# A triangular substitution moved to PSUM beside a four-bank pool, and its blocks stored block by block

## The chip, the cores and the metric

The kernel runs on one core of a Trainium2 chip. The metric is the device time of one execution in microseconds. Before the change it takes 909.23 us in the median of three runs (908.24 to 913.0).

## What is computed

Three stages follow one another. The first is a linear recurrence with a 40x40 state for each of 32 heads (4 batches of 8) over 768 steps:

```
for t in range(S):
    y[:, :, t] = einsum('bhd,bhde->bhe', rt, state)
    Sa = einsum('bhde,bhe->bhd', state, at)
    state = state * wt[:, :, None, :] - einsum('bhd,bhe->bhde', Sa, bt)
    state = state + einsum('bhd,bhe->bhde', vt, kt)
```

Its output, 3072 rows of 320, goes through two mixtures of 8 experts (320 to 1024 to 320, ReLU, the expert with the largest logit, its softmax weight as gate). In the first, rows with a negative skip score pass unchanged and the result is added to the row; in the second an expert takes at most `capacity` rows, and the rest give zero.

## The kernel before

**Tiling.** The recurrence is worked in chunks of 64 steps. A unit (`u`) is one chunk of the 8 heads of one batch; there are 48, and two batches alternate, so unit `u + 2` takes the state that unit `u` leaves. Within a unit the coupling of the steps is a triangular system of 64 rows for each head. Its inverse is put together from two 32x32 triangular blocks on the diagonal, inverted by substitution, and the block between them.

**The substitution.** Four units are a group; its 64 diagonal blocks (8 heads, 4 units, two blocks each) lie on 128 partitions, each block on two: one partition works the even columns of the inverse, the other the odd ones. `nt` holds a block (32x32) on each partition, `xs` its half of the growing inverse (16x32), both in SBUF and both read by VectorE (DVE). `solve_ops` (L277 to 301) is a generator of 62 steps for each group: for each of 31 columns one multiply (L290, the column of `xs` times the row of `nt` into `tmp`), and one add (L295, `tmp` onto `xs` in place). The sizes run from 16 to 136 elements a partition. Only in the first group are the larger steps cut in two.

**How it gets its data.** `scores` (L208) makes a unit's products on PE; ACT copies the negated ones to `abt` (L219), and one DMA stores them as 64 rows of 2048 bytes to `scr` in DRAM (L227). Once a group's four units are stored, `solve_in` (L247) loads `nt` with four DMAs of 32x32 runs of 128 bytes. `solve_new` (L257) makes a fresh `xs`: a memset and two memsets of its diagonal on GpSimd (POOL). At the group's end `solve_out` (L319) stores `xs` to `ttd` in DRAM with two DMAs, and `load_tt` (L329) brings it back as `tt` with four, in the layout that the matmuls need. `load_l21` (L268) loads the block between the diagonal ones from `scr`. All these DMAs are issued on SP's queue, in the order of the program.

**Order of the work.** It is written out by hand: what the program says first is issued first on each engine. `run` (L540) has one pass for each unit, with the units ahead (`v = u + 11`) being prepared beside the current one:

- on top: the DMAs due (`load_pre`, `load_duo`, the list `loads`, `load_post`), the transpose `tnat` of the next unit (L352, DVE, reads `tt`), `c1` and `stran` of this one (PE);
- `xmul` (L508, DVE), `decay` (L437, POOL, writes `spp`), `prep` (two scans on DVE, L177 and L192, around which POOL makes `kb`, L201, and `aks`, L203);
- `scores`, `uu`, `kbtr`, `gg` on PE, with ACT's copies between; `akmask` on POOL (L232, two selects);
- `t21a`, `c2`, `utr` (PE), `gmask` (L488, DVE), `yy` (PE), `state` (L428, DVE), `xx` every second pass, `t21b`.

Between these `fill(n)` puts n steps of the substitution on DVE (16 in a pass), and of smaller chores of the routing. A group's substitution takes up four passes; it ends in the pass with `u % 4 == 1`, its `tt` is loaded in the next pass and read by `tnat` in the one after.

**PSUM.** Eight banks: two for `scores`, `gg` and `warm` (pool `psA`), two shared by `kbtr`, `stran`, `xx` and the routing's counts (`psK`), two by `c1`, `uu`, `t21a`, `t21b`, `utr` (`psC`), and one each for the state's product `ps_s` and the output `ps_y`. The framework gives out the banks of a pool as the program's order frees them and makes the engines wait for the last reader.

**After the recurrence** PE runs the experts, with weights split into two parts, from about 470 us to the end.

Of the kernel before, what the change touches and what calls it, by code (L numbers as in the profile page):

```python
# [66 lines left out]
class Attention:  # L67
    def __init__(self, tc, ctx, aps, moe):
# [15 lines left out]
        self.psA = ep(tc.tile_pool(name="psA", bufs=2, space=P))  # L84
        self.psK = ep(tc.tile_pool(name="psK", bufs=2, space=P))
        self.psC = ep(tc.tile_pool(name="psC", bufs=2, space=P))
        self.psS = ep(tc.tile_pool(name="psS", bufs=1, space=P))

# [18 lines left out]

        self.ps_s = self.psS.tile([128, NP, D], F32, name="ps_s")
        self.ps_y = self.psS.tile([128, NP, C], F32, name="ps_y")
        self.in1b = [early([PR, NP, CW], F32, name=f"in1b{i}") for i in range(2)]  # L110
# [29 lines left out]
        self.warm(W0, zero[:, 0])  # L140
        self.later = [(V, self.ps_s), (V, self.ps_y), (V, self.tt[0]), (V, self.tt[1])]
        self.later += [(A, t[96:128]) for t in self.aks[E0:]]
# [65 lines left out]
    def scores(self, u):  # L208
        nc = self.nc
        X = self.U[u]  # L210
        ps = self.psA.tile([128, NP, 2, C], F32, name="psA")
        aks, kb = X["aks"], X["kb"]
        for p in range(NP):
            nc.tensor.matmul(ps[:, p], kb[:, p].rearrange("p x t -> p (x t)"),  # L214
                             aks[:, p].rearrange("p h t -> p (h t)"), start=True, stop=True)
        if u % 2 == 0:
            self.abt = self.pe.tile([128, NP * 2 * C], F32, name="abt", bufs=2)
        abt = self.abt[u % 2 * 64:u % 2 * 64 + 64]
        nc.scalar.activation(out=abt, in_=ps[64:128].rearrange("p a h t -> p (a h t)"), func=AF.Copy, scale=-1.0)  # L219
        for o, h in ((64, 0), (0, 1)):  # L220
            nc.scalar.copy(out=aks[o:o + 64, :, h], in_=ps[0:64, :, h])
        g = u // GU
        if u % GU == 0:
            scr = self.dr.tile([C, GU, H, C], F32, name="scr")
            self.grp[g] = dict(scr=scr)
        scr = self.grp[g]["scr"]
        nc.sync.dma_start(out=scr[:, u % GU].rearrange("s h t -> s (h t)"), in_=abt)  # L227

# [7 lines left out]
    def kbtr(self, u):  # L236
        nc = self.nc
        X = self.U[u]
        ps = self.psK.tile([128, NP, PR], F32, name="psK")
        for p in range(NP):  # L240
            nc.tensor.transpose(ps[:, p], X["kb"][0:PR, p].rearrange("p x t -> p (x t)"), self.ident[0:PR, 0:PR])
        kbs = self.pl.tile([128, NP, PR], F32, name="kbs", bufs=LEAD + 3)
        nc.scalar.copy(out=kbs, in_=ps)
        X["kbs"] = kbs


    def solve_in(self, g):  # L247
        nc = self.nc
        G = self.grp[g]
        scr = G["scr"].rearrange("s u h t -> s (u h) t")  # L250
        for par in range(2):
            for blk in range(2):
                o = par * 64 + blk * HB
                r = slice(blk * HB, blk * HB + HB)
                nc.sync.dma_start(out=G["nt"][o:o + HB], in_=scr[r, :, r].rearrange("s x t -> x s t"))

    def solve_new(self, G):  # L257
        nc = self.nc
        nt = self.pv.tile([128, HB, HB], F32, name="nt")
        xs = self.pv.tile([128, HB // 2, HB], F32, name="xs")  # L260
        nc.gpsimd.memset(xs, 0.0)
        xf = xs.rearrange("p c t -> p (c t)")
        for par in range(2):
            sl = slice(par * 64, par * 64 + 64)
            nc.gpsimd.memset(xf[sl, par:par + 15 * (HB + 2) + 1:HB + 2], 1.0)
        G.update(xs=xs, nt=nt)

    def load_l21(self, g):  # L268
        nc = self.nc
        G = self.grp[g]  # L270
        scr = G["scr"].rearrange("s u h t -> s (u h) t")
        l21 = self.p2.tile([128, GU * NP, HB], F32, name="l21")
# [4 lines left out]
    def solve_ops(self, g):  # L277
# [4 lines left out]
        def ops():  # L282
            for j in range(HB - 1):
# [13 lines left out]
                if j == HB - 2:  # L297
                    self.solve_out(g)
                yield
# [19 lines left out]
    def solve_out(self, g):  # L319
        nc = self.nc  # L320
        G = self.grp[g]
        xs = G["xs"]
        ttd = self.dr.tile([2 * GU * H, HB, HB], F32, name="ttd")
# [88 lines left out]
    def c2(self, u):  # L412
        nc = self.nc
        X = self.U[u]
        if u // IL % NCH == NCH - 1:
            return
        for p in range(NP):
            for r in (0, 64):
                nc.tensor.matmul(self.ps_s[r:r + D, p], X["kbs"][:, p, r:r + D], X["vu"][:, p, r // 64, 0:D], start=True, stop=True)

# [41 lines left out]
    def stran(self, u):  # L462
        nc = self.nc
        X = self.U[u]
        spp = self.spp[u % (2 * IL)]
        ps = self.psK.tile([128, NP, PR], F32, name="psSt", tag="psK")
        for p in range(NP):
# [22 lines left out]
    def yy(self, u):  # L490
        nc = self.nc
        X = self.U[u]

        for p in range(NP):
            for h in range(2):
                o = h * 64
                nc.tensor.matmul(self.ps_y[o:o + D, p], X["kbs"][:, p, o:o + D], X["g"][:, 2 * p + h],  # L497
                                 start=p == 0, stop=False, skip_group_check=True)
        for p in range(NP):
            for h in range(2):  # L500
                o = h * 64
                nc.tensor.matmul(self.ps_y[o:o + D, p], X["sde"][o:o + D, p], X["r"][o:o + D, h, p],  # L502
                                 start=False, stop=p == NP - 1, skip_group_check=True)

    def xmul(self, u):
        X = self.U[u]
        xt = self.xts[u // 2 % 2]
        self.nc.vector.tensor_tensor(out=xt[0:PR, :, (u % 2) * C:(u % 2) * C + C], in0=self.ps_y[0:PR], in1=X["pp"], op=ALU.mult)  # L508
        del self.U[u]
# [3 lines left out]
    def xx(self):  # L513
        nc = self.nc
        if self.xr is not None:
            t, xt = self.xr
            self.xr = None
            ps = self.psK.tile([128, NP, SELN], F32, name="psX", tag="psK")
            for p in range(NP):
# [20 lines left out]
    def run(self):  # L540
        self.todo, self.aux, self.sinks, self.loads = [], [], [], []
        self.xr, self.rate = None, 0.0
        begin = self.moe.setup()
        begins = [BG0, BG1, BG2] + [GU * g + 4 - LEAD for g in range(3, NG)]
        for u in range(-LEAD - 2, NU):
# [76 lines left out]
            if nxt == 0:  # L622
                self.warm(5, self.grp[0]["xs"].rearrange("p c t -> p (c t)"))
            if isn:
# [8 lines left out]
            for f in places:  # L633
                f()
            self.fill(FC)
            if on:
                self.state(u)
# [24 lines left out]
    def finish(self):  # L662

        self.last, self.placed = [], []
        last = self.psC.tile([128, NP, C], F32, name="psYl", tag="psC")
        self.nc.vector.memset(last, 0.0)
        self.xmul(NU - 3)
# [7 lines left out]
        self.xmul(NU - 2)  # L675
        self.ps_y = last
        self.yy(NU - 1)
# [130 lines left out]
class Moe:  # L808
# [44 lines left out]
    def route(self, rows, lg, valid, T, G, slack=0):  # L853
# [42 lines left out]
        def place():  # L896
            p = self.ps_pool(128, T * W).rearrange("p (t w) -> p t w", w=W)
            nc.tensor.matmul(p, self.tri, ohf, start=True, stop=False)
            nc.tensor.matmul(p, self.one, cs[:, 0:T], start=False, stop=True)
            ps.append(p)  # L900

# [533 lines left out]
def build(tc, aps):  # L1435
    nc = tc.nc
    with ExitStack() as ctx, tc.manual_schedule():
        moe = Moe(tc, ctx, aps)
        with ExitStack() as actx:
            att = Attention(tc, actx, aps, moe)  # L1440
            moe.ps_pool = lambda p, n: att.psK.tile([128, 512], F32, name="psR", tag="psK")[0:p, 0:n]
            att.run()
# [26 lines left out]
```

## Time and profile before

| | |
|---|---|
| median of the runs | 909.23 us |
| the profiled execution | 912.79 us |
| its span, first to last instruction | 911.1 us |
| mean granted clock of PE | 0.906 |
| PE busy | 818.9 us (90%) |
| DVE busy | 670.5 us (74%) |
| ACT busy | 483.7 us (53%) |
| POOL busy | 365.1 us (40%) |
| DMA | 138.45 MB, 199464 packets, 141425 of them under 512 B |

Times are microseconds unless marked ns. PE is the matmul engine, DVE VectorE, ACT ScalarE, POOL GpSimd, SP the queue that issues the DMAs. The profiled execution's span is one execution; a share of busy time is a mean over stages with different limits, so the steady stretch of the recurrence, 100 to 400 us, is read by itself. [...]

### The profile page before, as it was taken

How to read it: one execution, taken by the hardware profiler on the slowest of the kernel's cores; microseconds unless marked ns; L12 is line 12 of the kernel's file. 1: busy time of each engine (PE TensorE's matmuls, PEld its weight loads, DVE VectorE, ACT ScalarE, POOL GpSimd, SP SyncE). 2: the span in 40 equal slices, each digit the busy share in tenths (PEclk: the TensorE clock that was granted, in tenths of full speed). 3: DMA queues.
4: the chain of work that ended last, by engine and by line, in shares of the span. 5: the costliest groups of instructions: out<-in, count | busy, mean ns of one | idle time of the engine just before them, and what ended most of it. 6: DMA issues, size and time to landing. Idle time of an engine off the chain costs nothing.

```text
span 911.1 us, 24122 instructions
## 1 busy us (share of the span) xinstructions
PE 818.9 (90%) x9084; PEld 741.1 (81%) x9084; DVE 670.5 (74%) x1964; ACT 483.7 (53%) x1176; POOL 365.1 (40%) x487
## 2 busy tenths in 40 slices
PE   6657789898798988989999799999988999999995
PEld 5536678787687877878878599999988999999995
DVE  8999888999999999999745558887765444444441
ACT  5834565566566574766554255555634445455541
POOL 5743434445455454553022324334422333333321
PEclk7557797889888897999999799999999999999998
DMA  7989999987888978885573474554624245444310
GB/s 215 227 158 173 178 201 206 166 173 143 174 156 184 179 141 161 169 153 124 111 196 80 134 245 151 176 182 131 201 85 136 96 133 166 117 153 127 116 36 23
DMA packets 199464, 138.45 MB, mean 152 GB/s; under 512 B 141425, under 2 KB 182708, under 8 KB 199344
## 3 DMA queue, kind: packets, MB, share of 16 engines
q1 hardware_dynamic: 196000, 127.04, 61.3%
q0 software_dynamic: 3344, 9.83, 3.2%
q8 instruction: 74, 1.21, 0.6%
q14 instruction: 46, 0.38, 0.2%
HBM read 105.87 MB, written 32.43 MB: 152 GB/s over the span
## 4 chain that ended last, share of the span: by engine, by line
PE 47%; DVE 3%; POOL 2%; issue 2%; ACT 1%; DMA 1%; SPq 0%; POOLq 0%; ACTq 0%; DVEq 0%
PE psH L1154 18%; PE psY L1178 5%; PE psY L1180 5%; PE psY L1179 5%; PE psT L1133 2%; PE psG L481 1%; PE psY L1175 1%; PE psY L1176 1%; PE psR L1208 1%; PE ps_y L502 1%; PE psU L407 1%; PE ps_y L497 1%; PE psX L520 1%; DMA xslots<-rows,si 1%; PE psT L1197 1%
## 5 line engine op out<-in xcount | busy, mean ns | idle before, releaser
L290 DVE TENSOR_TENSOR tmp<-xs,nt 128x126 f32<-128x126 f32 (+27 forms) x391 | 180.8, 466 | 10.1 <-DMA nt<-scr 3.2
L1160 DVE SCALAR_TENSOR_TENSOR hl<-psH,hh 128x256 fp32r<-128x256 f32 (+1 forms) x136 | 64.9, 477 | 88.0 <-ACT hh L1158 86.3
L1158 ACT ACTIVATE hh<-psH 128x256 fp32r<-128x256 f32 (+1 forms) x136 | 61.4, 452 | 114.1 <-PE psH L1154 111.8
L1178 PE MATMUL psY<-w2h,hh 128*128 128x320 f32 x328 | 105.6, 322 | 0.0
L295 DVE TENSOR_TENSOR xs<-xs,tmp 128x126 f32<-128x126 f32 (+27 forms) x391 | 100.0, 260 | 6.7
L1180 PE MATMUL psY<-w2h,hl 128*128 128x320 f32 x328 | 101.8, 310 | 0.0
L1179 PE MATMUL psY<-w2l,hh 128*128 128x320 f32 x328 | 101.7, 310 | 0.0
L1154 PE MATMUL psH<-xh,w1h 128*128 128x256 f32 (+1 forms) x408 | 89.5, 329 | 1.8 <-ACT xh L1136 1.7
L214 PE MATMUL psA<-aks,kb 128*128 128x128 f32 x384 | 69.6, 340 | 22.2 <-POOL aks L203 18.0
L1154 PE MATMUL psH<-xl,w1h 128*128 128x256 f32 (+1 forms) x408 | 86.6, 322 | 0.0
L214 PEld LDWEIGHTS psA<-aks,kb 128*128 128x128 f32 x384 | 62.8, 248 | 25.4 <-POOL aks L203 20.1
L437 POOL TENSOR_TENSOR spp<-s,pc 104x320 f32<-104x320 f32 x44 | 32.2, 732 | 116.9 <-DVE s L428 49.7
L201 POOL TENSOR_TENSOR kb<-pre,q 104x512 f32<-104x512 f32 x40 | 47.4, 1185 | 75.8 <-PE psY L362 16.1
L203 POOL TENSOR_TENSOR aks<-pre,pp 104x512 f32<-104x512 f32 x48 | 58.5, 1219 | 42.8 <-DVE pp L192 34.7
L960 POOL DMA_INDIRECT out<-yo,ix x32 | 35.7, 1117 | 97.8 <-ACT yo L1231 47.4
L1154 PEld LDWEIGHTS psH<-xh,w1h 128*128 128x128 f32 x408 | 67.2, 195 | 5.3 <-ACT xh L1136 2.4
L1154 PEld LDWEIGHTS psH<-xl,w1h 128*128 128x128 f32 x408 | 67.3, 193 | 2.9
L481 PE MATMUL psG<-rb,vd 128*128 128x128 f32 x384 | 56.5, 292 | 11.6 <-DVE g L488 11.6
L1154 PE MATMUL psH<-xh,w1l 128*128 128x256 f32 (+1 forms) x272 | 65.2, 321 | 0.0
L377 ACT COPY tt<-psT 32x128 f32<-32x128 f32 x96 | 24.6, 256 | 75.6 <-PE psT L375 71.7
L1178 PEld LDWEIGHTS psY<-w2h,hh 128*128 128x128 f32 x328 | 62.1, 189 | 0.4
L1179 PEld LDWEIGHTS psY<-w2l,hh 128*128 128x128 f32 x328 | 62.1, 189 | 0.0
(172 smaller groups left out, 2040.5 us busy)
## 6 DMA issues: line engine op xcount, KB each, us to landing
pre<-pre SPq DMA_DIRECT2D x48, 523.2 KB
raw<-w SPq DMA_DIRECT2D x32, 512.0 KB
raw<-w SPq DMA_DIRECT2D x32, 480.0 KB
xslots<-mzero SPq DMA_DIRECT2D x11, 648.0 KB
scr<-abt SPq DMA_DIRECT2D x48, 128.0 KB
nt<-scr SPq DMA_DIRECT2D x48, 128.0 KB
vu<-vu SPq DMA_DIRECT2D x24, 256.0 KB
raw<-w SPq DMA_DIRECT2D x16, 320.0 KB
```

The costliest lines, as they stand in the source:

```text
L201: e.tensor_tensor(out=kb[0:PR].rearrange("p a x t -> p x a t"), in0=kbd, in1=qr.unsqueeze(1).to_broadcast([PR, 2, NP, C]), op=ALU.mult)
L203: nc.gpsimd.tensor_tensor(out=aks[0:PR], in0=a, in1=pp.unsqueeze(2).to_broadcast([PR, NP, 2, C]), op=ALU.mult)
L214: nc.tensor.matmul(ps[:, p], kb[:, p].rearrange("p x t -> p (x t)"), aks[:, p].rearrange("p h t -> p (h t)"), start=True, stop=True)
L290: nc.vector.tensor_tensor(out=tv[:, c:d], in0=xs[:, c:d, j:j + 1].to_broadcast([128, d - c, m]), in1=nt[:, j:j + 1, j + 1:HB].to_broadcast ...
L295: nc.vector.tensor_tensor(out=xs[:, c:d, j + 1:HB], in0=xs[:, c:d, j + 1:HB], in1=tv[:, c:d], op=ALU.add)
L481: nc.tensor.matmul(ps[:, 2 * p:2 * p + 2], vd[:, p].rearrange("q x t -> q (x t)"), r[:, :, p], start=True, stop=True)
L1154: nc.tensor.matmul(ps, a, b, start=j == 0, stop=j == 7)
L1158: nc.scalar.activation(out=hh[:, 0:n], in_=ps, func=AF.Relu)
L1160: nc.vector.scalar_tensor_tensor(out=o, in0=ps[:, s], scalar=0.0, in1=hh[:, s].bitcast(F32), op0=ALU.max, op1=ALU.subtract)
L1178: nc.tensor.matmul(ps[0:m], hh[:, s], bh[:, f], start=f == 0, stop=False)
L1179: nc.tensor.matmul(ps[0:m], hh[:, s], bl[:, f], start=False, stop=False)
L1180: nc.tensor.matmul(ps[0:m], hl[:, s], bh[:, f], start=False, stop=f == KF - 1)
```

## The change

`xs` moves into PSUM, in a pool of two banks (`psI`). Its start is kept once in SBUF (`xs0`), and ACT copies it into the bank for each group (`solve_new`); at the end ACT copies the result to SBUF for the DMAs (`solve_out`), which is now called later in the pass, after the last three fill steps, through the list `outs`. To free the banks, `psK`, `psC` and the two fixed banks become one pool of four, `psC`; the state's product and the output are allocated anew in each pass, and their first matmuls write 64 partitions in place of 40, so that the rows that are read with them are written. The counts of the routing are copied out of PSUM by ACT.

The scores are stored three times: the two diagonal blocks of each head to `scr`, head by head, and the upper 32 rows whole to `top`. `nt` is then loaded with two DMAs of one 4096-byte run a partition, and `l21` from `top`.

```diff
-        self.psK = ep(tc.tile_pool(name="psK", bufs=2, space=P))
-        self.psC = ep(tc.tile_pool(name="psC", bufs=2, space=P))
-        self.psS = ep(tc.tile_pool(name="psS", bufs=1, space=P))
+        self.psI = ep(tc.tile_pool(name="psI", bufs=2, space=P))
+        self.psC = ep(tc.tile_pool(name="psC", bufs=4, space=P))
...
-        self.ps_s = self.psS.tile([128, NP, D], F32, name="ps_s")
-        self.ps_y = self.psS.tile([128, NP, C], F32, name="ps_y")
+        self.xs0 = early([128, HB // 2, HB], F32, name="xs0")
...
+        G.memset(self.xs0, 0.0)
+        xf = self.xs0.rearrange("p c t -> p (c t)")
+        for par in range(2):
+            sl = slice(par * 64, par * 64 + 64)
+            G.memset(xf[sl, par:par + 15 * (HB + 2) + 1:HB + 2], 1.0)
...
-            scr = self.dr.tile([C, GU, H, C], F32, name="scr")
-            self.grp[g] = dict(scr=scr)
-        scr = self.grp[g]["scr"]
-        nc.sync.dma_start(out=scr[:, u % GU].rearrange("s h t -> s (h t)"), in_=abt)
+            scr = self.dr.tile([2, GU * H, HB, HB], F32, name="scr")
+            top = self.dr.tile([HB, GU, H, C], F32, name="top")
+            self.grp[g] = dict(scr=scr, top=top)
+        scr, top = self.grp[g]["scr"], self.grp[g]["top"]
+        for blk in range(2):
+            r = slice(blk * HB, blk * HB + HB)
+            nc.sync.dma_start(out=scr[blk, u % GU * H:u % GU * H + H].rearrange("h s t -> s h t"),
+                              in_=abt[r].rearrange("s (h t) -> s h t", h=H)[:, :, r])
+        nc.sync.dma_start(out=top[:, u % GU].rearrange("s h t -> s (h t)"), in_=abt[0:HB])
...
-        ps = self.psK.tile([128, NP, PR], F32, name="psK")
+        ps = self.psC.tile([128, NP, PR], F32, name="psK", tag="psC")
...
         for par in range(2):
-            for blk in range(2):
-                o = par * 64 + blk * HB
-                r = slice(blk * HB, blk * HB + HB)
-                nc.sync.dma_start(out=G["nt"][o:o + HB], in_=scr[r, :, r].rearrange("s x t -> x s t"))
+            nc.sync.dma_start(out=G["nt"][par * 64:par * 64 + 64], in_=G["scr"].rearrange("b x s t -> (b x) s t"))
...
         nt = self.pv.tile([128, HB, HB], F32, name="nt")
-        xs = self.pv.tile([128, HB // 2, HB], F32, name="xs")
-        nc.gpsimd.memset(xs, 0.0)
-        xf = xs.rearrange("p c t -> p (c t)")
-        for par in range(2):
-            sl = slice(par * 64, par * 64 + 64)
-            nc.gpsimd.memset(xf[sl, par:par + 15 * (HB + 2) + 1:HB + 2], 1.0)
+        xs = self.psI.tile([128, HB // 2, HB], F32, name="psI")
+        nc.scalar.copy(out=xs, in_=self.xs0)
...
                 if j == HB - 2:
-                    self.solve_out(g)
+                    self.outs.append(g)
...
-        xs = G["xs"]
+        xs = self.pv.tile([128, HB // 2, HB], F32, name="xs")
+        nc.scalar.copy(out=xs, in_=G["xs"])
...
+        self.ps_s = self.psC.tile([128, NP, D], F32, name="psS", tag="psC")
         for p in range(NP):
-            for r in (0, 64):
-                nc.tensor.matmul(self.ps_s[r:r + D, p], X["kbs"][:, p, r:r + D], ...)
+            for r, m in ((0, 64), (64, D)):
+                nc.tensor.matmul(self.ps_s[r:r + m, p], X["kbs"][:, p, r:r + m], ...)
...
-        ps = self.psK.tile([128, NP, PR], F32, name="psSt", tag="psK")
+        ps = self.psC.tile([128, NP, PR], F32, name="psSt", tag="psC")
...
+        X["py"] = ps = self.psC.tile([128, NP, C], F32, name="psY", tag="psC")
...
-            ps = self.psK.tile([128, NP, SELN], F32, name="psX", tag="psK")
+            ps = self.psC.tile([128, NP, SELN], F32, name="psX", tag="psC")
...
-                self.warm(5, self.grp[0]["xs"].rearrange("p c t -> p (c t)"))
+                self.warm(5, self.moe.zero[:, 0])
...
             self.fill(FC)
+            for g in self.outs:
+                self.solve_out(g)
+            self.outs = []
...
+            if G == 2 and self.paced:
+                c = t(Q * E, "pc").rearrange("p (t w) -> p t w", w=W)
+                nc.scalar.copy(out=c, in_=p)
+                p = c
```

## Rows read from the trace of the kernel before

**Rows 1.** 100 to 400 us: busy PE, PEld, DVE, ACT, POOL; PE clock; DMA share, GB/s.
```profile
100.00:400.00 300.00, 266.28 (x4214) 233.78 (x4212) 276.88 (x816) 175.55 (x513) 147.79 (x231) 0.87 0.89 171
```
**Rows 2.** Costliest groups: shapes, count, busy us, mean ns, idle before.
```profile
L290 DVE TENSOR_TENSOR tmp<-xs,nt 128x126 f32<-128x126 f32 (+27 forms) x391 | 180.8, 466 | 10.1 <-DMA nt<-scr 3.2
L295 DVE TENSOR_TENSOR xs<-xs,tmp 128x126 f32<-128x126 f32 (+27 forms) x391 | 100.0, 260 | 6.7
```
**Rows 3.** Order of time, DVE and POOL, 253 to 259: start, us, instruction.
```profile
253.20 0.78 POOL L437 TENSOR_TENSOR spp<-s,pc 104x320 f32<-104x320 f32 x1 [2.20 <-DVE xs L295]
253.40 0.65 DVE L290 TENSOR_TENSOR tmp<-xs,nt 128x58 f32<-128x58 f32 x1
...
254.38 0.69 DVE L177 TENSOR_TENSOR_SCAN q<-pre,one 104x264 f32<-104x264 f32 x1
...
255.20 1.17 POOL L201 TENSOR_TENSOR kb<-pre,q 104x512 f32<-104x512 f32 x1 [1.23 <-issue]
255.21 1.23 DVE L290 TENSOR_TENSOR tmp<-xs,nt 128x56 f32<-128x56 f32 x1
256.37 0.69 DVE L192 TENSOR_TENSOR_SCAN pp<-pre,in1b 104x264 f32<-104x264 f32 x1
...
257.14 1.19 POOL L203 TENSOR_TENSOR aks<-pre,pp 104x512 f32<-104x512 f32 x1 [0.77 <-DVE pp L192]
257.20 1.22 DVE L290 TENSOR_TENSOR tmp<-xs,nt 128x81 f32<-128x81 f32 x1
```
**Rows 4.** Groups kept apart by shape, DVE, to 470 us: busy us, mean ns.
```profile
L290 DVE TENSOR_TENSOR tmp<-xs,nt 128x115 f32<-128x115 f32 x11 | 3.0, 270 | 0.1
...
L290 DVE TENSOR_TENSOR tmp<-xs,nt 128x16 f32<-128x16 f32 x12 | 2.1, 175 | 0.3
```
**Rows 5.** Order of time, DVE and POOL, 89 to 93.5 us.
```profile
89.50 0.69 DVE L177 TENSOR_TENSOR_SCAN q<-pre,one 104x264 f32<-104x264 f32 x1
...
90.32 0.16 DVE L290 TENSOR_TENSOR tmp<-xs,nt 128x16 f32<-128x16 f32 x1
90.33 1.20 POOL L201 TENSOR_TENSOR kb<-pre,q 104x512 f32<-104x512 f32 x1 [0.80 <-PE psY L362]
90.44 1.65 DVE L192 TENSOR_TENSOR_SCAN pp<-pre,in1b 104x264 f32<-104x264 f32 x1
...
92.08 0.67 DVE L488 TENSOR_TENSOR g<-psG,cst 128x512 f32<-128x512 f32 x1
92.17 1.19 POOL L203 TENSOR_TENSOR aks<-pre,pp 104x512 f32<-104x512 f32 x1 [0.64 <-DVE xs L295]
92.68 0.72 DVE L290 TENSOR_TENSOR tmp<-xs,nt 128x31 f32<-128x31 f32 x1
```
**Rows 6.** As rows 4: instructions with an operand in PSUM, and one without.
```profile
L928 DVE TENSOR_TENSOR ok<-psR,ok 128x48 f32<-128x48 f32 x6 | 1.2, 201 | 0.7 <-PE psR L899 0.7
L932 DVE TENSOR_TENSOR u<-u,ok 128x48 f32<-128x48 f32 x6 | 1.2, 201 | 0.0
...
L130 DVE MEMSET ps_y<- 128x256 f32 x1 | 0.3, 272 | 0.0
```
**Rows 7.** From the last add to tnat: order of time, a wait's total, ACT's copy.
```profile
251.28 0.18 DVE L295 TENSOR_TENSOR xs<-xs,tmp 128x16 f32<-128x16 f32 x1
...
262.85 0.31 DVE L352 STREAM_TRANSPOSE tn<-tt 96x128 f32<-96x128 f32 x1 [0.31 <-DMA tt<-ttd]
...
DVE tn L352 <- DMA tt<-ttd: 17.5, 10, 3.9
...
L219 ACT ACTIVATE abt<-psA 64x512 f32<-64x512 f32 x48 | 28.5, 593 | 27.4 <-PE psA L214 16.0 <-issue 9.3
```
**Rows 8.** Order of time, PE, two iterations from 262.6 us: c1, gg, c1.
```profile
262.63 0.25 PE L395 MATMUL psZ<-vs,aks 128*64 128x40 f32 x1
...
265.76 1.08 PE L481 MATMUL psG<-rb,vd 128*128 128x128 f32 x8
...
277.68 0.25 PE L395 MATMUL psZ<-vs,aks 128*64 128x40 f32 x1
```

More of the change, by code (lines that the diff above doesn't have):

```diff
@@ L140, in __init__ @@
         self.warm(W0, zero[:, 0])
-        self.later = [(V, self.ps_s), (V, self.ps_y), (V, self.tt[0]), (V, self.tt[1])]
+        G.memset(self.xs0, 0.0)
[3 more added lines that the diff above has]
+            G.memset(xf[sl, par:par + 15 * (HB + 2) + 1:HB + 2], 1.0)
+        self.later = [(V, self.tt[0]), (V, self.tt[1])]
         self.later += [(A, t[96:128]) for t in self.aks[E0:]]
@@ L249, in solve_in @@
         G = self.grp[g]
-        scr = G["scr"].rearrange("s u h t -> s (u h) t")
         for par in range(2):
-            for blk in range(2):
-                o = par * 64 + blk * HB
-                r = slice(blk * HB, blk * HB + HB)
-                nc.sync.dma_start(out=G["nt"][o:o + HB], in_=scr[r, :, r].rearrange("s x t -> x s t"))
+            nc.sync.dma_start(out=G["nt"][par * 64:par * 64 + 64], in_=G["scr"].rearrange("b x s t -> (b x) s t"))
     def solve_new(self, G):
@@ L270, in load_l21 @@
         G = self.grp[g]
-        scr = G["scr"].rearrange("s u h t -> s (u h) t")
+        scr = G["top"].rearrange("s u h t -> s (u h) t")
         l21 = self.p2.tile([128, GU * NP, HB], F32, name="l21")
@@ L416, in c2 @@
             return
+        self.ps_s = self.psC.tile([128, NP, D], F32, name="psS", tag="psC")
         for p in range(NP):
-            for r in (0, 64):
-                nc.tensor.matmul(self.ps_s[r:r + D, p], X["kbs"][:, p, r:r + D], X["vu"][:, p, r // 64, 0:D], start=True, stop=True)
+            for r, m in ((0, 64), (64, D)):
+                nc.tensor.matmul(self.ps_s[r:r + m, p], X["kbs"][:, p, r:r + m], X["vu"][:, p, r // 64, 0:D], start=True, stop=True)
     def state(self, u):
@@ L492, in yy @@
         X = self.U[u]
+        X["py"] = ps = self.psC.tile([128, NP, C], F32, name="psY", tag="psC")
         for p in range(NP):
             for h in range(2):
-                o = h * 64
-                nc.tensor.matmul(self.ps_y[o:o + D, p], X["kbs"][:, p, o:o + D], X["g"][:, 2 * p + h],
+                o, m = h * 64, (64, D)[h]
+                nc.tensor.matmul(ps[o:o + m, p], X["kbs"][:, p, o:o + m], X["g"][:, 2 * p + h],
                                  start=p == 0, stop=False, skip_group_check=True)
@@ L501, in yy @@
                 o = h * 64
-                nc.tensor.matmul(self.ps_y[o:o + D, p], X["sde"][o:o + D, p], X["r"][o:o + D, h, p],
+                nc.tensor.matmul(ps[o:o + D, p], X["sde"][o:o + D, p], X["r"][o:o + D, h, p],
                                  start=False, stop=p == NP - 1, skip_group_check=True)
@@ L507, in xmul @@
         xt = self.xts[u // 2 % 2]
-        self.nc.vector.tensor_tensor(out=xt[0:PR, :, (u % 2) * C:(u % 2) * C + C], in0=self.ps_y[0:PR], in1=X["pp"], op=ALU.mult)
+        self.nc.vector.tensor_tensor(out=xt[0:PR, :, (u % 2) * C:(u % 2) * C + C], in0=X["py"][0:PR], in1=X["pp"], op=ALU.mult)
         del self.U[u]
@@ L540, in run @@
     def run(self):
-        self.todo, self.aux, self.sinks, self.loads = [], [], [], []
+        self.todo, self.aux, self.sinks, self.loads, self.outs = [], [], [], [], []
         self.xr, self.rate = None, 0.0
@@ L664, in finish @@
         self.last, self.placed = [], []
-        last = self.psC.tile([128, NP, C], F32, name="psYl", tag="psC")
-        self.nc.vector.memset(last, 0.0)
         self.xmul(NU - 3)
@@ L675, in finish @@
         self.xmul(NU - 2)
-        self.ps_y = last
         self.yy(NU - 1)
@@ L1440, in build @@
             att = Attention(tc, actx, aps, moe)
-            moe.ps_pool = lambda p, n: att.psK.tile([128, 512], F32, name="psR", tag="psK")[0:p, 0:n]
+            moe.ps_pool = lambda p, n: att.psC.tile([128, 512], F32, name="psR", tag="psC")[0:p, 0:n]
             att.run()
```

## The prediction

> **What bounds the kernel now.** I read the busy time by stretch first, then the costliest groups, then the order of time of one iteration on DVE and POOL together, then what each engine waits for. The expert stage from 470 us on is bound by PE and is not touched; the change lies in the attention stage. In its steady part, 100 to 400 us, DVE is busy 277 of 300 us and PE 266, at a mean granted clock of 0.87 of the upper level; ACT has 124 us free and POOL 152 [rows 1]. One iteration gives PE 132 matmul records and every second one 8 more, so 4214 records are 31 iterations of 9.7 us.
>
> The substitution is the largest DVE work: 391 multiplies of line 290 with 180.8 us and as many adds of line 295 with 100.0 us, on tiles of the same shapes [rows 2]. That a multiply costs 1.8 adds is the thing to explain. The order of time does: the multiply that begins beside POOL's kb takes 1.23 us and ends 0.07 us after kb does; the one beside aks 1.22 us; the one beside spp 0.65 us [rows 3]. At 16 and 115 elements, with POOL quiet, a multiply takes 175 and 270 ns, that is 160 ns and 0.96 ns an element [rows 4]; by that line the three would have cost 0.21, 0.24 and 0.22 us. So a DVE instruction that reads two SBUF operands stands still until the POOL instruction beside it is done. The mask product of line 488, one operand in PSUM and one in SBUF, began 0.09 us before an aks, ran 0.6 us beside it and took its usual 0.67 us; the multiply that followed was held at once, 0.72 us for 31 elements [rows 5]. The held operand pair is what the change breaks up.
>
> **What the change removes.** All multiplies together have 12 x 2856 = 34,272 elements, so undisturbed they cost 391 x 0.160 + 34,272 x 0.00096 = 95.5 us: 85.3 us too much. The adds by the same line are 4.5 us too long. Together 90 us of DVE standing still. With one operand in PSUM these stalls should go. How the 90 us divide: I paired each long multiply with the POOL instruction beside it: 33 beside kb, 40 beside aks (the first at 32.4 us, the last at 406.1 us), 29 beside spp, the rest beside the two selects of akmask. At 1.02, 0.98 and 0.43 us [rows 3] these are 34, 39 and 12 us, and 5 us remain for the selects.
>
> **What is late next, kb.** kb starts 0.13 us after the scan of line 177 ends. Behind the multiply stands the scan of line 192, which reads two SBUF operands too. The trace holds the case after the change already: at 90.3 us the multiply slipped in ahead of kb (0.16 us), and the scan stood instead, 1.65 us against 0.69 us. From the end of the first scan to the end of the second: 1.90 us there [rows 5], 1.99 us where the multiply was held [rows 3]. So of kb's 34 us only 40 x 0.09 = 4 us come back. After aks and spp the next DVE instructions are substitution steps and PSUM readers, about 1.2 us of them, so those stalls go whole. DVE gains 39 + 12 + 5 + 4 = 60 us. In the first iterations and after 400 us it isn't always the last to arrive; I count 55.
>
> **What an operand in PSUM costs DVE.** Reading: line 928 reads PSUM and takes 201 ns, line 932 with the same shape reads SBUF alone and takes 201 ns [rows 6]. Nothing per instruction. [...] Writing: no row has a DVE instruction that reads and writes the same bank, as line 295 now does. [...] From below it costs nothing (I see no reason for a gain); from above, if read and write took turns, 0.96 ns more for each of 34,272 elements, 33 us. [...]
>
> **What is late next, tt.** The solved matrix goes to DRAM and comes back as tt, and the transpose of line 352 waits for it: 17.5 us in 10 of 12 groups [rows 7]. In the group shown the last add ends at 251.46 us, which releases the store, and line 352 starts at 262.85 us, held by the load [rows 7]: 11.4 us, taken by DMA work issued in one order on SP's queue behind the store (pre, vs, vu, tt). [...] Meanwhile DVE's way to line 352 gets shorter by what aks, spp and the selects took in that stretch, 1.5 us. Each of some ten groups waits 2.2 us more: +22 us.
>
> **PSUM pool.** One pool of four banks replaces two pools of two and two fixed banks. Free banks are handed out oldest first, in the order of the program. Working that through: psX is no problem (its bank comes free before it is wanted), but the bank of the state product, held until line 428, goes in every second iteration to c1 of the next one and in the others to stran. PE then can't run ahead of DVE's state into the next iteration; today it may go on to c2. Behind it on PE stand scores, uu, kbtr and gg, and DVE's mask waits for gg. At full clock c1 to gg takes 4.2 us (262.63 to 266.84) [rows 8], DVE's work between the two about 6 us, so it is hidden; at the lower level it takes 8 us and DVE stands 2 us. With a mean clock of 0.87 a quarter of the stage is at that level, some 8 of 31 iterations, and half of them may be caught by DVE's waits for tt: +8 us.
>
> **Taken as nothing.** ACT's 24 copies of about 0.6 us: 14 us in its 124 us of idle time; uncovered they would cost 14 us. POOL's memsets go, but POOL isn't last. Stores by block: two more DMA issues a unit, and 48 x 512 runs of 128 bytes more; nt: 48 loads of 1024 short runs become 24 of 64 long ones, 24,576 short runs fewer in all. The multiply waits for nt only 3.2 us in total [rows 2], so that is the most it can bring; SP's extra issues stand where it waits anyway. If the small stores were late, nt would be, and the same row says there are some us of slack. The matmuls of c2 and yy on 64 instead of 40 output rows move the same columns: nothing.
>
> **Sum.** -55 + 22 + 8 = -25 us. The profiled execution took 912.79 us (span 911.1), so 888; the median of the runs shown is 909.23, so **884 us**, its own range 868 to 900.
>
> **Rivals.** (1) PE takes over. Its two iterations at full clock take 15.05 us [rows 8], 7.5 each, 8.6 at the stage's clock; 1.1 us of waiting makes up the 9.7. If half of the waiting stays and the pool's coupling adds to it, the stage gives 12 us: 897. For it: PE is 89% busy; against it: the faster DVE takes away waits, and the clock falls behind waits. (2) kb's stall goes too, or tt hides: the adds and multiplies regroup so that the scan starts after kb, or the DMA runs shorter for its 24,576 fewer short runs: 25 to 30 us more, 856. Against it are the 1.65 us scan and the chain of 11.4 us. (3) Slower: line 295 in place in one PSUM bank. It decides from 0.7 ns per element on; at the upper bound of 33 us the sum is +8, 917; with more waiting for PE, 925. [...] (4) The change doesn't free the operand: multiplies stay long, the longer tt chain stays, some 5 us slower, 914. Against it stands line 488.
>
> **How the numbers follow.** Chances: forecast 0.50, (1) 0.18, (2) 0.12, (3) 0.15 (0.03 of it the fixed price), (4) 0.05. About 0.5% is what a measurement here tells from no change: 904.7 to 913.8 us. Faster: nearly all of the forecast and (2), most of (1): 0.75. Same: the rest of (1), half of (4): 0.10. Slower: 0.15. For 8 in 10 the range goes from within (2) to (4): 852 to 914; the ends hold the unknown price of line 295 up to about 30 us.
>
> **What would show it.** Line 290 with a mean near 245 ns, without executions near 1.2 us: the stall is gone; if it keeps 460 ns, (4). Line 192 with many executions of 1.3 to 1.7 us and a mean above 1.2 us: kb's part moved. Line 295 with a mean near 250 ns: no price in PSUM; near 340 ns: (3). The wait of line 352 for tt near 40 us in all; if it stays at 17, that term was wrong. PE's waits for lines 428 and 352, with the granted clock behind them: the pool's coupling. The prediction is wrong if DVE's busy time in 100 to 400 us falls and the stage isn't shorter.

## The result: 1.2% slower

Median 922.2 us of 4 runs (921.1 to 925.2) against 910.2 us beside them; ratio 1.012, 95% interval 1.008 to 1.016. The profiled execution took 925.21 us (span 923.5, mean granted clock 0.922). The forecast was 884 us.

Changed kernel, groups of instructions on DVE; columns as in [rows 2]:

```profile
L296 DVE TENSOR_TENSOR psI<-psI,tmp 128x126 f32<-128x126 f32 (+27 forms) x391 | 97.5, 249 | 7.4
L291 DVE TENSOR_TENSOR tmp<-psI,nt 128x126 f32<-128x126 f32 (+27 forms) x391 | 93.3, 243 | 30.9 <-DMA nt<-scr 23.6
L195 DVE TENSOR_TENSOR_SCAN pp<-pre,in1b 104x264 f32<-104x264 f32 x48 | 62.5, 1302 | 0.3
```

DVE did what was forecast: the multiply fell from 466 to 243 ns, the add in place in PSUM has a mean of 249 against 260 ns [rows 2], and the scan took over kb's stall. The same stretch as in [rows 1]:

```profile
100.00:400.00 300.00, 260.19 (x4144) 229.98 (x4144) 230.84 (x826) 182.51 (x527) 139.39 (x208) 0.90 0.85 171
```

DVE is busy 231 in place of 277 us, and PE's records are fewer, not more: the stage became no shorter. Waits over the whole span (engine, what waited, for what: us in total, times, longest):

```profile
DVE tn L354 <- DMA tt<-ttd: 36.1, 11, 5.1
DVE tmp L291 <- DMA nt<-scr: 23.6, 6, 7.3
```
```profile
PE psSt L471 <- ACT zbd L401: 13.3, 16, 0.9
PE psZ L397 <- ACT tt L379: 11.4, 17, 1.1
```

The wait for tt is that of [rows 7], 17.5 us there, and was forecast at 40. The others were not forecast: nt (3.2 us in [rows 2]) and two waits of PE that the kernel before has nowhere. How the latter look, in order of time:

```profile
281.17 0.44 PE L377 MATMUL psT<-tt,y 32*32 32x32 f32 x16
281.66 0.52 ACT L379 COPY tt<-psT 32x128 f32<-32x128 f32 x2 [2.07 <-PE psT L377]
...
282.23 0.25 PE L397 MATMUL psZ<-vs,aks 128*64 128x40 f32 x1 [0.62 <-ACT tt L379]
...
283.03 0.28 ACT L400 COPY zbd<-psZ 64x160 f32<-64x160 f32 x1 [0.84 <-PE psZ L398]
283.34 0.29 ACT L401 COPY zbd<-psZ 64x160 f32<-64x160 f32 x1
...
283.72 0.49 PE L471 MATMUL psSt<-cst,spp 104*128 104x104 f32 x2 [0.82 <-ACT zbd L401]
```

c1 (psZ) needs nothing of t21b's result, nor stran (psSt) of c1's, yet each waits until ACT has emptied what stands before it: they are in one bank. In the built program c1 has the bank that t21b took just before it in 18 of 48 passes, and stran that of c1 in 17; the waits are 17 and 16. In the program of the kernel before it happens in no pass.

The stage by stretches, us, from the starts of c1 (first column: c1 of unit 0) and of the experts' first product, one profiled execution each; in brackets per iteration:

| kernel | to unit 0 | 0 to 12 | 12 to 36 | 36 to experts | experts start |
|---|---|---|---|---|---|
| before | 74.5 | 119.6 | 220.9 (9.21) | 106.8 | 521.8 |
| after | 74.3 | 122.8 | 222.2 (9.26) | 117.5 | 536.7 |
| e1_pool | 75.0 | 117.5 | 227.7 (9.49) | 115.5 | 535.7 |
| e2_store | 75.6 | 122.7 | 221.9 (9.24) | 106.1 | 526.2 |
| e3_oldstore | 76.0 | 114.1 | 221.9 (9.25) | 115.5 | 527.5 |
| e4_ownbanks | 75.6 | 115.5 | 211.2 (8.80) | 105.3 | 507.6 |
| e7_five | 74.3 | 121.3 | 212.0 (8.83) | 110.5 | 518.0 |
| e9_out_behind | 75.3 | 117.6 | 220.9 (9.21) | 105.7 | 519.5 |
| e11_scan_later | 74.2 | 116.7 | 208.4 (8.68) | 107.9 | 507.2 |
| e12_scan_nopre | 73.7 | 90.3 | 183.9 (7.66) | 106.5 | 454.3 |
| e13_after_nopre | 71.9 | 100.0 | 218.1 (9.09) | 119.2 | 509.2 |
| e14_before_nopre | 73.4 | 106.4 | 224.8 (9.37) | 107.2 | 511.8 |

The recurrence goes on until the experts start, at 521.8 us before the change, and not only to about 470 us. In the changed kernel 21 of the 24 iterations from unit 12 to 36 take a regular 8.9 to 10.0 us, with DVE free for a fifth of the time. Of the 14.9 us by which the experts start later, 10.7 lie in the last stretch, in which only the last group is solved, so that DVE has little to gain there. The two waits of PE come to 3.0 us in it. DVE's waits for the routing (lines 936 and 988 here, 928 and 980 before) grow in it from 12.0 to 22.0 us. e1_pool has 8.7 of the 10.7 us and e7_five 3.6, so most of it comes with the pool; by what way it comes stays open.

### The profile page after: what moved, and what is told of

Its sections match the earlier page's. It is cut to its first block, busy times and chain, and to the rows that moved or that the text cites. A ratio compares the mean times of both kernels' runs of the same rounds, so it can differ in the third digit from the quotient of the medians.

```text
span 923.5 us, 24241 instructions
## 1 busy us (share of the span) xinstructions
PE 814.0 (88%) x9084; PEld 739.6 (80%) x9084; DVE 613.5 (66%) x1961; ACT 497.1 (54%) x1211; POOL 356.0 (39%) x454
## 4 chain that ended last, share of the span: by engine, by line
PE 68%; DMA 12%; DVE 8%; ACT 7%; issue 3%; SPq 1%; POOL 1%; ACTq 0%; POOLq 0%; DVEq 0%
PE psH L1162 18%; PE psY L1186 5%; PE psY L1188 5%; PE psY L1187 5%; DMA pre<-pre 4%; PE psG L484 3%; PE psA L217 3%; PE psU L409 3%; PE psY L501 2%; PE psX L524 2%; PE psY L506 2%; PE psSt L471 2%; DMA tt<-ttd 2%; PE psZ L397 2%; PE psS L422 2%
## 5 line engine op out<-in xcount | busy, mean ns | idle before, releaser
L291 DVE TENSOR_TENSOR tmp<-psI,nt 128x126 f32<-128x126 f32 (+27 forms) x391 | 93.3, 243 | 30.9 <-DMA nt<-scr 23.6
L296 DVE TENSOR_TENSOR psI<-psI,tmp 128x126 f32<-128x126 f32 (+27 forms) x391 | 97.5, 249 | 7.4
L204 POOL TENSOR_TENSOR kb<-pre,q 104x512 f32<-104x512 f32 x40 | 47.0, 1176 | 84.7 <-PE psY L364 18.8
L195 DVE TENSOR_TENSOR_SCAN pp<-pre,in1b 104x264 f32<-104x264 f32 x48 | 62.5, 1302 | 0.3
L1188 PEld LDWEIGHTS psY<-w2h,hl 128*128 128x128 f32 x328 | 61.5, 188 | 0.0
```

Source lines behind the costliest of these rows:

```text
L195: nc.vector.tensor_tensor_scan(ppr.rearrange("p a i -> p (a i)"), w[:, ::-1], in1b.rearrange("p a i -> p (a i)"), 0.0, ALU.mult, ALU.add)
L204: e.tensor_tensor(out=kb[0:PR].rearrange("p a x t -> p x a t"), in0=kbd, in1=qr.unsqueeze(1).to_broadcast([PR, 2, NP, C]), op=ALU.mult)
L291: nc.vector.tensor_tensor(out=tv[:, c:d], in0=xs[:, c:d, j:j + 1].to_broadcast([128, d - c, m]), in1=nt[:, j:j + 1, j + 1:HB].to_broadcast ...
L296: nc.vector.tensor_tensor(out=xs[:, c:d, j + 1:HB], in0=xs[:, c:d, j + 1:HB], in1=tv[:, c:d], op=ALU.add)
L1188: nc.tensor.matmul(ps[0:m], hl[:, s], bh[:, f], start=False, stop=f == KF - 1)
```

## The experiments

Theory A: the four-bank pool ties PE to ACT's evictions. B: the new storage makes nt late. C: the longer way of tt. Later D: DMA's load. Ratios are to the kernel before, with 95% intervals; its median beside them was 910 to 912 us. The edits are shown shortened, some of them in words.

**e1_pool**: before, with the pool alone.

```diff
-psK 2 banks, psC 2, ps_s 1, ps_y 1; xs in SBUF
+psC 4 banks for all of these; xs in SBUF
```


> The kernel before with nothing but the four-bank pool (with its two wider products and the counts copied out of PSUM by ACT); xs stays in SBUF, the storage is the old one. Theory A (the shared pool ties PE to ACT's evictions, the 25 us of new PE waits for lines 379 and 401 after the change): 15 to 25 us slower than before, 925 to 935 us, and the same two waits of 0.6 to 0.8 us stand in PE's list. Theory B (the new storage makes nt late) and theory C (the later copy out makes tt late): within 4 us of before.

927.0 us, ratio 1.018 (1.014 to 1.021): 16 us slower. The waits are there, and in this program c1 has the bank of t21b in 16 passes and stran that of c1 in 11:

```profile
PE psZ L391 <- ACT tt L373: 10.1, 16, 0.7
PE psSt L465 <- ACT zbd L395: 8.2, 10, 0.8
```

**e2_store**: before, with the new storage and load alone.

```diff
-scr <- abt, 64 rows; nt by four loads
+scr <- abt, two diagonal blocks; top <- abt; nt by two loads
```


> The kernel before with nothing but the storage block by block and the one-run load of nt. Theory B: DVE's wait for nt grows from 3.2 us to about 20 us and, as DVE bounds the kernel before, the time by 12 to 18 us, 922 to 928 us. Theory A: the wait for nt stands beside other waits, at most 5 us slower.

915.9 us, ratio 1.005 (1.002 to 1.008): 4.5 us slower, the wait for nt 10.1 us in place of 3.2. The time is what A expected (at most 5 us); the wait lies between the two.

**e3_oldstore**: the changed kernel with that part undone.

> The changed kernel with the old storage (one store of 64 rows a unit, four loads of nt, l21 from the same rows). Theory B: the wait for nt (23.6 us, 6 times) falls below 5 us and the time by 15 to 20 us, 903 to 908 us. Theory A: the wait falls too, but PE's waits for evictions stay and the time falls by no more than 6 us, 916 to 922 us.

917.7 us, ratio 1.007 (1.004 to 1.009), some 5 us under the changed kernel: A's size. The wait for nt fell only to 15.6 us, where B expected under 5: most of it isn't the storage's. PE's two waits stay (11.2 us 18 times, 12.3 us 15 times), as A expected.

**e4_ownbanks**: xs in PSUM, but with the other pools of the kernel before.

```diff
-ps_s and ps_y in a bank each; xs in SBUF
+ps_s and ps_y in one bank; xs in one bank, copied in behind the copy out of the last
```


> The kernel before with xs in PSUM, in one bank in place of two (a group's xs is copied in behind the copy out of the group before), the freed bank got by putting the state's product and the output in one; all other pools and the storage as before. Theory A: without the shared pool the forecast's gain appears, -55 us of stalls and +22 us for tt, and some 1 us a group for the one bank: 880 to 892 us. Theory C (the later tt and ACT's longer queue eat the gain whatever the pools are): 900 to 912 us, with a wait for tt of 36 us or more.

899.9 us, ratio 0.988 (0.984 to 0.992). Without the shared pool the edit gains, but 11 us, not the 20 to 30 of A alone. By its numbers this is C's edge (900 to 912 us, a wait for tt of 36 us or more): the pool isn't the only thing that kept the gain away. (The shared bank has a price of its own: line 436 waits 6.1 us for the output's products.) tt is now what the engines stand for, in DVE's list and in PE's:

```profile
DVE tn L360 <- DMA tt<-ttd: 36.9, 10, 7.0
```
```profile
PE psY L370 <- DVE tn L360: 17.3, 12, 5.2
```

**e5_early_tt and e6_after_early**: in e4_ownbanks and in the changed kernel, the substitution ends earlier and tt is loaded at once.

```diff
-FB = 5; FC = 3
+FB = 6; FC = 4
             self.fill(FA)
+            self.out()    # solve_out, before scores
+            self.load()   # load_tt
```


> The kernel of run e4_ownbanks, in which DVE waits 37 us for tt and PE 17 us for the transposes behind it, with the substitution two steps a pass faster, so that it ends before the scores of its pass, and with xs copied out, stored and tt loaded right there instead of at the end of the pass and in the next one. Theory C (with its own banks the kernel is held by the way of tt through DRAM): the wait for tt falls from 37 us to under 10 us, PE's for the transpose to under 8 us, and the time from 900 to 875 to 888 us. Rival (PE has taken over, my first rival): the waits fall as well, but others take their place, and the time falls by less than 6 us.

> The changed kernel, four-bank pool and all, with the same earlier end of the substitution, earlier copy out, store and load of tt. Theory A (PE's waits for ACT's evictions set the pace of the changed kernel): the wait for tt falls from 36 us to under 12 us, PE's waits for lines 379 and 401 stay at 20 us or more, and the time falls by no more than 8 us, 914 to 922 us. Theory C alone (tt is what lost the gain): 895 to 908 us.

911.7 us, ratio 1.002 (1.000 to 1.004), and 932.5 us, ratio 1.026 (1.023 to 1.029): each 10 to 12 us slower than its base by the medians. In e5_early_tt the wait for tt fell to 6.4 us, and ACT, which now comes to the copy out before the last add is done, holds vu and with it PE:

```profile
ACT xs L335 <- DVE psI L302: 43.6, 10, 15.6
```
```profile
PE ps_b L432 <- ACT vu L422: 30.6, 9, 4.9
```

(15.6 of ACT's us are the first group's, at 61 us, ahead of unit 0.) In e6_after_early the wait for tt went as well (9.4 us), and nt's rose to 41.4 us. The edit was badly placed, so this refutes C only together with e9_out_behind.

**e7_five**: the changed kernel with one bank for xs and five in the pool.

```diff
-psI bufs=2; psC bufs=4
+psI bufs=1; psC bufs=5   (xs copied in behind the copy out)
```


> The changed kernel with one bank for xs and five in the shared pool. As built, c1 then never gets the bank that t21b filled just before it, nor stran that of c1 just before; in the changed kernel 17 and 16 iterations do. Theory A: PE's waits for ACT's copies of tt and zbd (11.4 and 13.3 us) fall below 5 us together, and the time by 8 to 15 us, 907 to 914 us; tt and nt still late. Rival (it is not the number of banks but the state's product and the output in the pool, or the clock): same time within 4 us.

902.6 us, ratio 0.993 (0.991 to 0.996): 19 us under the changed kernel by the medians, more than the 8 to 15 expected. c1 and stran get the bank just filled in no pass, and the two waits are gone (psZ 2.6 us for nothing that the profile shows, psSt 1.5 us for POOL), while tt and nt are as late as in the changed kernel:

```profile
DVE tn L357 <- DMA tt<-ttd: 43.9, 12, 5.9
DVE tmp L294 <- DMA nt<-scr: 22.3, 6, 8.9
```

The state's product and the output, with their wider first matmuls (in the changed kernel 237 ns for c2 and 234 for yy, beside 217 and 229 with 40 rows), are still in the pool here, so they aren't what costs by themselves. That is the pool's cost shown from the other side of e1_pool.

**e8_nopc**: the changed kernel without ACT's copy of the counts.

> The changed kernel without ACT's copy of the routing's counts; DVE reads them in PSUM as before. DVE's wait of 8.8 us for that copy goes back to one for PE of about 6 us, but the bank of the counts is held longer, with PE's products behind it. Theory A: within 4 us of the changed kernel, either way. Rival (the copy on ACT is a cost by itself): 5 us or more faster.

928.4 us, ratio 1.018 (1.015 to 1.022): 6 us slower than the changed kernel, just outside A's 4. The longer held bank turns up in the same two waits, now 23 and 19 times (14.4 and 15.6 us). The copy was worth its ACT time.

**e9_out_behind and e10_nt_first**: e5_early_tt with the copy out behind vu and kbs; and with nt loaded there too.

```diff
             self.fill(FA)
-            self.out()
-            self.load()
...
                 self.gg(u - 1)
+            self.out()
+            self.load()   # e9: load_tt alone; e10: solve_in as well
```


> As run e5_early_tt (substitution two steps a pass faster, tt loaded in the pass in which it ends), but with the copy out behind vu and kbs in ACT's order, where DVE's last add is done, instead of ahead of them. In e5_early_tt the wait for tt was gone, and ACT stood 28 us for the last add, PE 31 us for vu behind it. Theory C2 (that stand on ACT is what ate the gain; the way of tt is what holds e4_ownbanks): ACT's wait for the add falls below 8 us, PE's for vu below 6 us, tt's stays below 10 us, and the time is 880 to 892 us. Rival (PE has taken over, and the clock gives back what waits go): 896 to 908 us, near e4_ownbanks or above.

> As run e9_out_behind, with the load of nt issued in the same place too, right behind the fourth unit's store, instead of in the next pass behind that pass's other loads. If nt's wait (10 to 15 us in the two kernels that this one comes from) holds the substitution: that wait falls below 4 us and the time is 3 to 8 us under e9_out_behind. Rival: SP stands for the store, the next loads are late, and the time is the same or longer.

912.8 us, ratio 0.999 (0.996 to 1.002), and 911.6 us, ratio 0.996 (0.993 to 1.000). In e9_out_behind ACT's stand after the first group and PE's for vu are gone (ACT 17.5 us, 15.1 of them the first group's), tt waits 11.5 us; yet it is 13 us slower than e4_ownbanks. In e10_nt_first nt still waits 32.4 us. C2 falls. In e9_out_behind DVE waits for nt instead, and PE for vs, which SP issues behind the early loads:

```profile
DVE tmp L297 <- DMA nt<-scr: 39.3, 8, 10.8
DVE tn L365 <- DMA tt<-ttd: 11.5, 8, 2.5
```
```profile
PE psZ L408 <- DMA vs<-vs: 16.8, 5, 5.3
```

Whatever is asked for earlier, another transfer is late. That is not the form of my rival (PE); it made me look at DMA.

**e11_scan_later and e15_after_scan**: in e4_ownbanks and in the changed kernel, three steps put ahead of the scan, so that kb is done when it starts.

```diff
-        self.fill(1)     # before the scan of pp
+        self.fill(FA)
...
-            self.fill(FA)     # after prep
+            self.fill(1)
```


> The kernel of run e4_ownbanks with three of the four steps that follow the second scan put before it, so that POOL's kb is done when the scan starts. Theory (the scan of pp took over the multiply's stall beside kb): its mean falls from 1311 ns to 800 to 900 ns and DVE's busy time by 18 to 24 us. On the time: if DVE still set the pace, 10 us or more under e4_ownbanks, 885 to 890 us; if PE and tt do, within 5 us of it, 895 to 905 us.

> The changed kernel with three of the steps that follow the second scan put before it, the edit that brought e4_ownbanks 13 us. The scan's mean falls from 1302 to 800 to 900 ns. Theory A (PE behind ACT's evictions sets the pace): at most 4 us faster. Rival (DVE's chain still counts in the changed kernel): 8 to 13 us faster.

The scan falls to 812 ns in the one and 788 ns in the other:

```profile
L200 DVE TENSOR_TENSOR_SCAN pp<-pre,in1b 104x264 f32<-104x264 f32 x48 | 39.0, 812 | 0.3
```

With banks of its own the kernel goes to 891.1 us, ratio 0.974 (0.970 to 0.978), the fastest of all (9 us under e4_ownbanks by the medians, 1.4% by the ratios); in the changed kernel to 920.7 us, ratio 1.010 (1.006 to 1.015), no gain that can be told. So DVE's chain still counts where PE isn't tied (10 us or more was expected if it set the pace). The traces can't show where: the profiled executions of the two kernels took 895.1 and 896.0 us, the one of e11_scan_later being at the slow end of its runs. As expected of A in the changed kernel: PE keeps its waits (12.6 us 15 times, 12.1 us 18 times).

**e12_scan_nopre, e13_after_nopre, e14_before_nopre**: the loads of pre from the fifth unit on are left out.

```diff
+        if 4 <= u < NU:
+            self.pre[u] = self.keep[u % 4]   # data of the first four units
```


> The kernel of run e11_scan_later without the loads of pre from the fifth unit on (523 KB a unit, about a quarter of the stage's DMA work); later units compute on the data of the first four. Theory D (DMA, busy 0.91 of 100 to 400 us, makes tt and nt late): the waits for tt and nt (59 us there) fall below 20 us and the time by 20 to 30 us, 860 to 872 us. Rival P (PE's own work of 7.5 to 8.5 us an iteration is the floor): the waits move, the time falls by no more than 8 us. Rival L (the chain through DRAM is latency, not load): waits and time as before, within 5 us.

> The changed kernel without the loads of pre from the fifth unit on, as in e12_scan_nopre. Theory D with A: the waits for nt and tt (24 and 36 us) fall below 20 us together, but PE's waits for evictions stay, and the time falls by 5 to 12 us. If DMA alone had lost the gain: 20 us or more.

> The kernel before without the loads of pre from the fifth unit on, as in e12_scan_nopre. DVE with its stalls sets the pace there, with 17.5 us of waiting for tt: by theory D 5 to 15 us faster; if DMA's load has no part, within 4 us of before.

With such data the rows crowd on few experts and the kernel goes through its general path for that (11.4 ms after the recurrence), so their whole times (11.9 ms) say nothing; the stretches of the table do. In e12_scan_nopre the experts start 53 us earlier than in e11_scan_later, half of it before unit 12 (26 us) and half after (24.5 us). Stretch 100 to 400 us and DVE's wait of e12_scan_nopre:

```profile
100.00:400.00 300.00, 292.83 (x5257) 256.62 (x5257) 255.29 (x1009) 221.10 (x646) 152.42 (x225) 0.99 0.66 139
```
```profile
DVE tn L362 <- DMA tt<-ttd: 20.5, 11, 5.7
```

Against e11_scan_later in the same stretch and list:

```profile
100.00:400.00 300.00, 273.58 (x4441) 242.76 (x4442) 226.05 (x869) 191.34 (x552) 143.79 (x214) 0.87 0.91 178
```
```profile
DVE tn L360 <- DMA tt<-ttd: 52.7, 12, 7.1
DVE tmp L297 <- DMA nt<-scr: 15.6, 4, 6.0
```

nt's wait is gone, tt's is 20.5 us, and PE is busy 293 of 300 us: here PE is the bound, at 7.66 us an iteration and a granted clock of 0.99. D holds: with less DMA work the transfers come in time. How much of the 53 us is theirs is less clear. In units 12 to 36 PE is busy 195.3 of 208.4 us in e11_scan_later, at a granted clock of 0.91, and 179.0 of 183.9 us in e12_scan_nopre, at 1.00, with as many records: of the 24.5 us there, 16.4 are PE's own instructions getting shorter and 8.1 its waits. Whether the clock rose because the waits went, no run here separates. In e13_after_nopre the waits for tt and nt fall just so (15.0 and 0.5 us), the first twelve units gain 23 us, and from 12 to 36 the iteration goes only from 9.26 to 9.09 us, since PE's waits are all there:

```profile
PE psSt L473 <- ACT zbd L403: 14.2, 17, 1.1
PE psZ L399 <- ACT tt L381: 11.7, 17, 1.2
```

In e14_before_nopre the first twelve units gain 13 us and the rest nothing (9.37): there DVE with its stalls is the bound, busy 291 of 300 us in 100 to 400 us. The experts start 10 us earlier in e14_before_nopre, as expected, and 27.5 us earlier in e13_after_nopre, where 5 to 12 were expected, and 20 or more if DMA alone had lost the gain. Without these loads the changed kernel starts its experts 2.6 us before the kernel before, with them 14.9 us behind it; its last stretch is 12.0 us longer all the same. So the loss in the first 36 units shows only where DMA is nearly full (4.5 us with these loads, at shares of 0.85 and 0.89 in 100 to 400 us; a gain of 13.1 us without, at 0.55 and 0.57).

**e16_scan_store**: e11_scan_later with the new storage.

> The kernel of run e11_scan_later with the new storage, block by block, and nt loaded as one run a partition. By theory D (DMA's load sets the pace there) the 24,576 short packets fewer would bring 3 to 10 us, 881 to 888 us, with DMA's share in 100 to 400 us below 0.88. Theory B (what counts is when the last store has landed, and three stores of short runs land later than one): the wait for nt grows from 15.6 us to 22 us or more, and the time by 3 to 8 us, 894 to 899 us.

901.7 us, ratio 0.989 (0.985 to 0.994): 10 us slower than e11_scan_later by the medians, nt's wait 24.5 us. B, by a little more than expected, even where DMA counts. The packets, some 23,400 fewer (176,041 against 199,464 in all in the kernel before), don't pay. In the third group the last store that nt needs is issued at 84.7 us in place of 80.9, and the multiply that waits for nt begins at 93.5 in place of 92.3; why the stores come that much later on SP stays open.

## Why the prediction was wrong, step by step

The sum was -25 us and the change measured +12. Of these 37 us, 22 are in the stalls and tt, 8 to 11 in the pool, and 4.5 or more in the stores.

- **The stalls, -55 us.** Right as an account of DVE: busy time fell from 670.5 to 613.5 us, line 291 has 243 ns (245 forecast). Wrong as a term of the sum, and this is the largest miss: it was counted whole on the path. In e4_ownbanks, without pool and storage, the stalls, the longer way of tt and the banks' own rearrangement come to -11 us together, where -55 + 22 were -33.
- **What is late next was DMA.** The failed step of that term. [rows 1] had DMA at 0.89, in the same row as DVE's 277 us, and I read only the engines. The step from the kernel before to e11_scan_later brings the experts 14.6 us forward; with a quarter of the DMA work gone in both (e14_before_nopre, e12_scan_nopre; DMA's share 0.57 and 0.66) it brings 57.5 us, with a higher granted clock in it.
- **kb's stall moves to the scan.** Right: 1302 ns, over 1200. That it could be had for nothing by three steps in another place (e11_scan_later, 9 us) I didn't see.
- **Price of PSUM.** Right but for some 3 us: the multiply fits the line from SBUF's undisturbed sizes (243 ns, 244 by the line), and the add in place, freed of its stalls, is some 8 ns longer than at the same shape in SBUF. The memset of [rows 6] pointed the same way: 272 ns for 256 elements into PSUM, beside 278 ns for 264 into SBUF (line 130 of the kernel before). No run shows the fixed price of an instruction that has 0.03 of the chances: lines 928 and 932 take 201 ns alike, and the multiply and the add have means of 243 and 249 ns in PSUM. Rivals 3 and 4 fall with these rows.
- **tt, +22 us.** The size of the wait was right (36.1 us for 40), its place in the sum was not: taking most of it away gained nothing (e9_out_behind), as the next transfer was late instead. No run shows the 2.2 us a group of which the term is made; the traces have a wait longer by 18.6 us in all, and 590 ns for ACT's copy out of the bank (line 324 of the changed kernel, 12 times).
- **The pool, +8 us.** A failed step, and the one that makes the change slower than the kernel before: the other parts, -11 and +4.5 us, would be -6.5. "psX is no problem" rested on my assumption that free banks are given out oldest first. As built, the bank of the state's product, that of the output and psX's are held across the passes' border, and in 17 passes, each behind a psX, three products in a row (t21b, c1, stran) go through the one bank that is left. PE waits for ACT, not for DVE's state as I had it. The 8 us from c1 to gg at the lower clock were my estimate: with the clock at 0.50 for most of the way (228 to 234 us in the kernel before) it took 6.9 us, from 228.31 to 235.20. Measured: 16 us alone (e1_pool), 19 us taken away (e7_five). The built program and the trace agree: 18 and 17 passes in which a product gets the bank just filled, 17 and 16 waits. The waits aren't the whole of it: of the 13.9 us by which the experts start later in e1_pool, 8.7 lie in the last stretch, by a way that stays open.
- **Stores and nt, nothing.** Wrong by 4.5 us (e2_store), 5 (e3_oldstore), 10 (e16_scan_store). I had "if the small stores were late, nt would be" and set it aside for some slack that the 3.2 us of [rows 2] were to prove; they only showed that DVE was late too.
- **Rival 1, PE takes over (897 us)** has the number of e4_ownbanks and part of its cause. PE's busy share of units 12 to 36 is 90% in the kernel before, 91% in e4_ownbanks and 94% in e11_scan_later, near the full; its longest wait in the last two, in 100 to 400 us, is for tn, which waits for tt (15.6 and 13.8 us). In e12_scan_nopre it is 97%, at 7.66 us an iteration where [rows 8] gave 7.5 at full clock.

The parts, -11, +16 (alone) to 19 (taken away) and +4.5 us, come to +9.5 to +12.5; the change measured +12. That they add up so well is partly luck: the storage cost 10 us in e16_scan_store, and the waits take each other's place.

## What to carry to other kernels

Before an engine's stalls are counted as a gain, read what else is close to full in the same stretch, DMA's share too: here an iteration of units 12 to 36 took 9.2 us with DVE's stalls, 9.1 with the pool and less DMA work, and 8.7 with neither stalls nor pool but all the DMA work, so that freeing one showed the next within 0.6 us. Banks freed by merging pools aren't free (here 16 us, e1_pool): list from the built program who had each bank before whom, and count the places where an engine gets back the bank that it has just filled. A wait that goes away has been worth nothing if the list of waits shows its length under another name.

## What the runs showed of the hardware

A DVE add that reads and writes one PSUM bank in place takes some 8 ns longer than in SBUF: that is the median over the 42 shapes, and it is longer in 37 of them. The means over all shapes, 249 against 260 ns, hide it, since the 260 hold stalls. At 128x121, for one, it is 292 against 284 ns in the mean of 11.

nt as 64 runs of 4096 bytes a load came little sooner than as 1024 of 128: where the multiply waits for it, 4.6 to 8.9 us after the first issue in e16_scan_store (6.3 in the mean of six), 6.4 to 8.1 us in e11_scan_later (7.4 in the mean of four). In the third group it was issued 2.3 us later (87.5 against 85.3 us).

PE's granted clock in 100 to 400 us isn't ordered by its busy time: 0.87 with 274 us (e11_scan_later), 0.95 with 268 us (e13_after_nopre), 0.99 with 293 us (e12_scan_nopre); what sets it stays open. In the kernel before it is at 1.00 in 105 of the 150 stretches of 2 us there and at 0.50 in 31. It was at 0.50 from 228 to 234 us, after PE had been busy for 1.85 of the 4 us from 222, and from 252 to 258 us, after none of the 2 us from 248; after 1.00 of the 2 us from 242 it stayed at 1.00.
